# The first batch's opening: order of loads, who adds two half tiles, and block 0's scores in two groups

## The chip, the cores and the metric

The program runs on one core of one Trainium2 chip. The time is device microseconds (us) of the whole program, the median of three runs; a trace of one further execution is read beside it. On a core, TensorE (PE in the profile) multiplies matrices into PSUM, VectorE (DVE), ScalarE (ACT) and GpSimd (POOL) work elementwise, and SyncE (SP) issues the DMAs. Each engine works through its own instructions in order.

## What is computed

Four batches of attention over spatially reduced keys, followed by a small MLP on each batch's best 128 rows:

```
kv_pool = kv.reshape(B, H//4, 4, W//4, 4, C).mean(axis=(2, 4))    # 16 taps to one row
k = v = kv_pool.reshape(B, -1, C) @ w_sr                          # 768 keys a batch
s = (q @ k.T) / sqrt(C); a = exp(s - s.max(-1)); a /= a.sum(-1) + 1e-9
x = a @ v                                                         # 12288 rows a batch
out = x; out[top 128 rows by x @ w_gate] += sigmoid(x @ w_gate) * (relu(x @ w1) @ w2)
```

B is 4, C is 128; q has 12288 rows in each batch, kv has 384 x 32 positions.

## The kernel before

**Tiling.** The 768 keys of a batch are six tiles of 128. A tile's raw data (`kv_raw`, 128 channels x 2 halves x 64 keys x 16 taps, 1 MB) is added over the 16 taps into `pooled` (128 x 128). `project` (line 150) multiplies `pooled` by `w_k` (the keys, transposed) and by `w_sr` (the values) into one PSUM bank. ACT copies that to `kv_proj`, and each key tile is split for exactness into `kh` (a 32-bit matmul type), `kb` and `kl` (bf16: the value itself and what `kh` misses): `split_k` (line 154), two ACT casts and one POOL subtraction. Queries are split likewise by `split_q` (line 319) into `qh` (ACT) and `ql` (POOL), for two blocks at a time.

**Blocks.** The 192 blocks of 256 queries run in one loop. `S` (line 332) makes the scores of a block, 2 x 768 columns, as four parts of three matmuls each (`qh` x `kh`, `qb` x `kl`, `ql` x `kb`). `s_max` is one DVE reduction over all 1536 columns into `m`; ACT takes the exponential; the probabilities are cut into a high and a low half (`hl`, ACT and POOL), turned by DMA transposes and partly by PE (`turn_pe`, which is why `ident` in `cst` is needed), and `AV` multiplies them with the values four blocks later (`LAG` is 4). The values need scales from the whole batch first: `v_gate` (a product with the gate's weights, kept in `cst`), `v_max` and `v_peak` on DVE, then `v_split`, which writes `vx`.

**The opening, batch 0** (`first_keys`, line 214, called at line 604). Here DVE alone adds the tiles, half a tile (64 keys) an instruction. Batches 1 to 3 get theirs in the loop by `next_keys`, where POOL adds in seven instructions a tile. `first_values` (line 251) is a task whose steps the loop takes at named points: its first step at "g" of block 0, after `s_max(0)`, its second at "d" at the end of block 0, ahead of `s_max(1)`.

**What sets the order.** `InOrder` (line 37) ties every PE, DVE, ACT and POOL instruction to the one before it in the program's text, so that an engine never takes a later instruction ahead of an earlier one. The DMAs that SP issues stand in the text's order too. Buffers order the rest: `kv_raw` has three (`kvp`), so tiles 3, 4 and 5 are loaded into the buffers of tiles 0, 1 and 2 and the load waits until those have been read; `pooled` has two (`kvs`), so tile 4's sum is written where tile 2's was, and waits for tile 2's projection. Accesses to one PSUM bank of a tile are also put in order. `warm` (line 210) issues filler matmuls on PE, whose results nobody reads. In the page and the trace nearly every instruction has line 52, the helper's.

Of the kernel before, what the change touches and what calls it, by code (L numbers as in the profile page):

```python
# [6 lines left out]
F32 = mybir.dt.float32  # L7
# [6 lines left out]
AF = mybir.ActivationFunctionType  # L14
ALU = mybir.AluOpType
AX = mybir.AxisListType
# [3 lines left out]
P = 128  # L20
# [3 lines left out]
KT = M // P  # L24
TAPS = R * R
CHUNK = 2048
# [3 lines left out]
BLK = QT * P  # L30
# [36 lines left out]
def attention_topk_mlp(ctx, tc, a, outs, capacity):  # L67
    nc = tc.nc
    pe, dve, act, pool = (InOrder(tc, e) for e in (nc.tensor, nc.vector, nc.scalar, nc.gpsimd))
    SK = 1.0 / float(C) ** 0.5 / TAPS  # L70

    const = ctx.enter_context(tc.tile_pool(name="const", bufs=1))
    kvp = ctx.enter_context(tc.tile_pool(name="kvp", bufs=3))
    kvs = ctx.enter_context(tc.tile_pool(name="kvs", bufs=2))
# [10 lines left out]
    ps_o = ctx.enter_context(tc.tile_pool(name="ps_o", bufs=1, space=PSUM))  # L85

    w_sr = const.tile([P, C], F32, name="w_sr")
    nc.sync.dma_start(out=w_sr, in_=a["w_sr"])
    w_k = const.tile([P, C], F32, name="w_k")
    act.activation(w_k, w_sr, AF.Copy, scale=SK)  # L90
    cst = const.tile([P, 5 * P], F32, name="cst")
    ident, tri, jrow, wg = (cst[:, i * P:(i + 1) * P] for i in range(4))
    jcol, base = cst[:, 4 * P:4 * P + 1], cst[:, 4 * P + 1:4 * P + 3]
# [2 lines left out]
    tri16 = const.tile([P, P], BF16, name="tri16")  # L96
# [3 lines left out]
    s_flat = [x.rearrange("p k q -> p (k q)") for x in s_buf]  # L100
# [3 lines left out]
    banks = [o_two[:, j] for j in range(QT)]  # L104
# [14 lines left out]
    def load_kv(b, kc, parts=1, t=None):  # L119
        late = t is not None  # L120
        if not late:
            t = kvp.tile([P, 2, P // 2, TAPS], F32, name="kv_raw")
        n = 2 // abs(parts)
        for i in range(abs(parts)):
            if parts > 0 or late == (i > 0):
                nc.sync.dma_start(out=t[:, i * n:(i + 1) * n], in_=a["kv"][:, b, kc, i * n:(i + 1) * n])
        return t

    qraw = {}

    def load_q(b, ch, lo=0, hi=CHUNK):
        if (b, ch) not in qraw:
            qraw[b, ch] = qp.tile([P, CHUNK], F32, name="q_raw")
        nc.sync.dma_start(out=qraw[b, ch][:, lo:hi], in_=a["q"][:, b, ch, lo:hi])
# [3 lines left out]
    def new_keys(b):  # L138
        kvset[b] = {
            "kh": keys.tile([P, M], F32R, name="kh"),  # L140
            "kl": keys.tile([P, M], BF16, name="kl"),
            "kb": keys.tile([P, M], BF16, name="kb"),
            "raw": keys.tile([P, KT, 2, P], F32, name="kv_proj"),
            "vw": keys.tile([P, KT], F32, name="vw"),
            "mx": keys.tile([P, 4], F32, name="mx"),
            "vx": keys.tile([P, 2, KT, VC], F16, name="vx"),
            "sg": keys.tile([P, 4], F32, name="sg"),
        }

    def project(pooled, ps):  # L150
        pe.matmul(ps[:, 0], w_k, pooled, start=True, stop=True)
        pe.matmul(ps[:, 1], pooled, w_sr, start=True, stop=True)

    def split_k(b, lo, hi, part):
        kv = kvset[b]
        kh, kl, kb = (kv[k][:, lo * P:hi * P].rearrange("p (t k) -> p t k", k=P) for k in ("kh", "kl", "kb"))
        raw = kv["raw"][:, lo:hi, 0]
        if part == 0:
            act.copy(kh, raw)
            act.copy(kb, raw)  # L160
        else:
            kv["split"] = hi
            pool.tensor_tensor(out=kl, in0=raw, in1=kh.bitcast(F32), op=ALU.subtract)

    def v_gate(b, kc, v=None):
        u = kvs.tile([P, C], F32, name="vw_prod")
        dve.scalar_tensor_tensor(out=u, in0=kvset[b]["raw"][:, kc, 1] if v is None else v, scalar=1.0, in1=wg, op0=ALU.mult, op1=ALU.mult, accum_out=kvset[b]["vw"][:, kc:kc + 1])

    def v_max(b, pair):
        kv = kvset[b]  # L170
        dve.tensor_reduce(out=kv["mx"][:, pair:pair + 1], in_=kv["raw"][:, 2 * pair:2 * pair + 2, 1], axis=AX.XY, op=ALU.max, apply_absolute_value=True)

    def v_peak(b):
        mx, vw = kvset[b]["mx"], kvset[b]["vw"]
        dve.tensor_reduce(out=mx[:, 0:1], in_=mx[:, 0:3], axis=AX.X, op=ALU.max)
        dve.tensor_reduce(out=mx[:, 1:2], in_=vw, axis=AX.X, op=ALU.max, apply_absolute_value=True)
# [33 lines left out]
    def warm(n, ps):  # L210
        for _ in range(n):
            pe.matmul(ps, ones16, ones16, start=True, stop=True)

    def first_keys():
        new_keys(0)
        load_q(0, 0, 0, 2 * BLK)
        raws = [load_kv(0, kc) for kc in range(3)]
        nc.sync.dma_start(out=cst, in_=a["cst"])
        raws += [load_kv(0, kc, 2) for kc in range(3, KT)]
        load_q(0, 0, 2 * BLK, CHUNK)  # L220
        split_q(0, 0)
        kv = kvset[0]
        for kc in range(KT):
            pooled = kvs.tile([P, P], F32, name="pooled")
            for h in range(2):
                dve.tensor_reduce(out=pooled[:, h * P // 2:(h + 1) * P // 2], in_=raws[kc][:, h], axis=AX.X, op=ALU.add)
            if kc == 4:
                dve.tensor_copy(tri16, tri)
            if kc > 1:
                v_gate(0, kc - 2)  # L230
            if kc == 3:
                v_max(0, 0)
            ps = banks[kc % 2][:, 0:2 * P].rearrange("p (a b) -> p a b", a=2)
            if kc < KT - 1:
                project(pooled, ps)
                act.copy(kv["raw"][:, kc], ps)
                split_k(0, kc, kc + 1, 0)
                split_k(0, kc, kc + 1, 1)
            else:
                warm(4, banks[0][:, 0:P])  # L240
                project(pooled, ps)
                kh, kl, kb = (kv[k][:, kc * P:(kc + 1) * P] for k in ("kh", "kl", "kb"))
                dve.tensor_copy(kh, ps[:, 0])
                act.copy(kb, ps[:, 0])
                dve.tensor_tensor(out=kl, in0=ps[:, 0], in1=kh.bitcast(F32), op=ALU.subtract)
                act.copy(kv["raw"][:, kc, 1], ps[:, 1])
                warm(8, banks[1][:, 0:P])
        S(0)
        S(1)

    def first_values():
        yield "g"
        v_gate(0, KT - 2)
        v_max(0, 1)
        yield "d"
        v_gate(0, KT - 1)
        v_max(0, 2)
        v_peak(0)
        yield from v_split(0)

# [54 lines left out]
    qsplit = {}  # L315
# [3 lines left out]
    def split_q(b, blk):  # L319
        ch, h = divmod(blk, BPC)  # L320
        raw = qraw[b, ch][:, h * BLK:(h + 2) * BLK]
        qh = qs.tile([P, 2 * BLK], F32R, name="qh")
        ql = qs.tile([P, 2 * BLK], BF16, name="ql")
        act.copy(qh, raw)
        pool.tensor_tensor(out=ql, in0=raw, in1=qh.bitcast(F32), op=ALU.subtract)
        for i in range(2):
            h, l = (x[:, i * BLK:(i + 1) * BLK] for x in (qh, ql))
            qsplit[b, blk + i] = h, h.bitcast(BF16).rearrange("p (q s) -> p q s", s=2)[:, :, 1], l
# [3 lines left out]
    def S(n, parts=(0, 1, 2, 3), apart=()):  # L332
        b, blk = blocks[n]
        kh, kl, kb = (kvset[b][x] for x in ("kh", "kl", "kb"))
        qh, qb, ql = qsplit[b, blk]
        assert b == 0 or kvset[b].get("split") == KT
        for part in parts:
            lo, hi, j, k0 = ((0, 512, 0, 0), (512, 768, 0, 512), (768, 1024, 1, 0), (1024, 1536, 1, 256))[part]
            q = slice(j * P, (j + 1) * P)
            k = slice(k0, k0 + hi - lo)  # L340
            low, high = [(qb, kl), (ql, kb)], [(qh, kh)]
            for i, (w, x) in enumerate(high + low if part in (2, 0) else low + high):
                r = pe.matmul(s_flat[n % 2][:, lo:hi], w[:, q], x[:, k], start=(i == 0), stop=(i == 2))
                for y in apart:
                    tc.declare_no_dep(r.ins, y, reason="other banks")
# [256 lines left out]
    blocks = [(b, blk) for b in range(B) for blk in range(NBLK)]  # L602

    first_keys()
    nc.sync.dma_start(out=w1, in_=a["w1"])
    nc.sync.dma_start(out=w2, in_=a["w2"].rearrange("(t f) d -> f t d", f=P))
# [12 lines left out]
    def at_point(point):  # L619
        advance(vals, point)  # L620
        advance(prep, point)
        advance(select, point)

    start(vals, first_values())
    nb = len(blocks)
    LAG = 4
    for i in range(nb):
        old = i >= LAG
        b, blk = blocks[i]
# [56 lines left out]
    b = blocks[n][0]  # L686
# [168 lines left out]
    for m in range(n - 3, n + 1):  # L855
        out(m)
        norm(m)
        if m > n - 2:
            lo = blocks[m][1] * QT
# [99 lines left out]
```

## Time and profile before

| | |
|---|---|
| median of 3 runs | 961.53 us (959.38 to 965.91) |
| the profiled execution's own time | 964.65 us |
| its span | 962.7 us |
| mean granted TensorE clock | 0.991 |
| busy: PE, ACT, POOL, DVE | 93%, 78%, 78%, 71% |

A row of the timeline gives the start, the time (of all instructions merged into the row), the engine, the line, the operation and what it writes and reads with its shape; in brackets stands how long the engine was idle before it and what ended that. A merged row ("x2") begins with its first instruction. A granted clock of 1.00 is TensorE's full speed. The span begins at the first instruction, which is also where the stretches below are counted from.

### The profile page before, as it was taken

How to read it: one execution, taken by the hardware profiler on the slowest of the kernel's cores; microseconds unless marked ns; L12 is line 12 of the kernel's file. 1: busy time of each engine (PE TensorE's matmuls, PEld its weight loads, DVE VectorE, ACT ScalarE, POOL GpSimd, SP SyncE). 2: the span in 40 equal slices, each digit the busy share in tenths (PEclk: the TensorE clock that was granted, in tenths of full speed). 3: DMA queues.
4: the chain of work that ended last, by engine and by line, in shares of the span. 5: the costliest groups of instructions: out<-in, count | busy, mean ns of one | idle time of the engine just before them, and what ended most of it. 6: DMA issues, size and time to landing. Idle time of an engine off the chain costs nothing.

```text
span 962.7 us, 25910 instructions
## 1 busy us (share of the span) xinstructions
PE 894.8 (93%) x10093; PEld 730.6 (76%) x10093; DVE 686.0 (71%) x1575; ACT 754.1 (78%) x1181; POOL 753.7 (78%) x577
## 2 busy tenths in 40 slices
PE   3889999998999999999899999999999999899976
PEld 2668887787777777888687877888778877688765
DVE  6446666675777777787757877787777878688743
ACT  2568888786888777888788888888888988799941
POOL 1478898887798887899779989898878787588752
PEclk9999999999999999999999999999999999999999
DMA  9799999999989999999999999999999999999990
GB/s 361 211 206 207 240 240 221 230 233 236 218 178 217 236 211 236 238 217 236 240 193 205 215 238 236 225 206 205 197 206 205 238 239 232 223 252 224 231 179 27
DMA packets 600574, 211.47 MB, mean 220 GB/s; under 512 B 532320, under 2 KB 582624, under 8 KB 599680
## 3 DMA queue, kind: packets, MB, share of 16 engines
q1 hardware_dynamic: 600128, 209.12, 106.2%
q8 instruction: 80, 1.31, 0.6%
q0 software_dynamic: 320, 0.66, 0.2%
q14 instruction: 46, 0.38, 0.1%
HBM read 52.10 MB, written 25.49 MB: 81 GB/s over the span
## 4 chain that ended last, share of the span: by engine, by line
PE 56%; DMA 12%; ACT 9%; issue 6%; POOL 6%; DVE 5%; SPq 0%; POOLq 0%; DVEq 0%; another core or an unknown queue 0%; ACTq 0%
PE s L52 30%; PE o_two L52 26%; DMA at<-hl 12%; ACT am L52 4%; DVE m L52 2%; ACT hl L52 2%; POOL hl L52 2%; POOL ql L52 2%; POOL kv_sum L52 2%; DMA xe<-out,idx 1%; ACT qh L52 1%; DVE kv_raw L52 1%; ACT s L52 0%; POOL out L52 0%; ACT at L52 0%
## 5 line engine op out<-in xcount | busy, mean ns | idle before, releaser
L52 POOL TENSOR_TENSOR hl<-am,hl 128x1280 bf16<-128x1280 f32 x192 | 504.5, 2628 | 149.2 <-ACT hl L52 62.6
L52 PEld LDWEIGHTS <-at 128*128 128x128 f16 (+1 forms) x6912 | 417.2, 97 | 77.9 <-DMA at<-hl 28.0
L52 PE MATMUL o_two<-vx,at 128*128 128x130 f16 x6804 | 435.7, 220 | 24.1 <-DMA at<-hl 18.4
L52 ACT ACTIVATE am<-s,m 128x512 f32<-128x512 f32 (+1 forms) x528 | 358.5, 707 | 59.9 <-DVE m L52 34.4
L52 DVE TENSOR_REDUCE m<-s 128x2 f32<-128x1536 f32 x192 | 337.1, 1756 | 35.7 <-PE s L52 35.3
L52 PE MATMUL s<-kl,qh 128*128 128x512 bf16 (+1 forms) x768 | 253.4, 333 | 0.0
L52 PE MATMUL s<-kh,qh 128*128 128x512 f32 (+1 forms) x768 | 251.8, 409 | 1.5 <-DVE mg L52 1.5
L52 PE MATMUL s<-kb,ql 128*128 128x512 bf16 (+1 forms) x768 | 248.6, 327 | 2.3 <-POOL ql L52 1.8
L52 ACT CAST hl<-am 128x1280 f16<-128x1280 f32 x192 | 241.9, 1260 | 6.1
L52 PEld LDWEIGHTS s<-kh,qh 128*128 128x128 f32 x768 | 131.5, 191 | 31.6 <-DVE mg L52 1.9
L52 DVE TENSOR_TENSOR at<-s,at 128x256 bf16<-128x256 f32 x144 | 61.2, 425 | 103.1 <-ACT at L52 95.5
L52 POOL TENSOR_TENSOR ql<-q_raw,qh 128x512 bf16<-128x512 f32 x96 | 122.5, 1276 | 7.0 <-ACT qh L52 7.0
L52 PEld LDWEIGHTS <-qh 128*128 128x128 bf16 x768 | 75.3, 98 | 62.7 <-issue 61.8
L52 ACT CAST at<-s 128x256 f16<-128x256 f32 x144 | 53.6, 372 | 75.7 <-PE s L52 75.7
L52 DVE TENSOR_TENSOR x<-o_two,rz 128x260 f32<-128x260 f32 x189 | 81.0, 429 | 10.0
L52 PEld LDWEIGHTS <-ql 128*128 128x128 bf16 x768 | 76.2, 99 | 8.4 <-POOL ql L52 5.6
L52 DVE TENSOR_SCALAR rz<-o_two,sg 128x2 f32<-128x2 f32 x189 | 41.0, 217 | 39.6 <-PE o_two L52 39.2
L52 PE MATMUL s<-cst,am 128*128 128x128 f32 x288 | 56.4, 278 | 6.2 <-ACT am L52 5.8
L52 ACT CAST qh<-q_raw 128x512 fp32r<-128x512 f32 x96 | 59.0, 615 | 1.3 <-DMA q_raw<-in_q 1.3
L52 POOL TENSOR_TENSOR kv_sum<-kv_raw 128x256 f32<-128x256 f32 x72 | 52.3, 727 | 0.0
L52 PEld LDWEIGHTS s<-cst,am 128*128 128x128 f32 x288 | 34.5, 141 | 14.7 <-ACT am L52 13.2
L52 DVE RECIPROCAL rz<-rz 128x2 f32<-128x2 f32 x192 | 31.9, 166 | 6.6
(156 smaller groups left out, 502.7 us busy)
## 6 DMA issues: line engine op xcount, KB each, us to landing
out<-x SPq DMA_DIRECT2D x96, 256.0 KB, 2.9
q_raw<-in_q SPq DMA_DIRECT2D x93, 256.0 KB, 3.5
kv_raw<-in_kv SPq DMA_DIRECT2D x36, 512.0 KB, 6.4
kv_raw<-in_kv SPq DMA_DIRECT2D x6, 1024.0 KB
at<-hl SPq DMA_TRANSPOSE x384, 3.9
w<-in_w SPq DMA_DIRECT2D x2, 512.0 KB
q_raw<-in_q SPq DMA_DIRECT2D x1, 768.0 KB
cst<-in_cst SPq DMA_DIRECT2D x1, 320.0 KB
```

The costliest lines, as they stand in the source:

```text
L52: r = f(*args, **kwargs)
```

## The change

All of it lies in `first_keys` and `first_values`. Tile 0's first half is loaded ahead of all else, then `w_sr`, tile 0's second half, tiles 1 and 2, and only then the first 512 query columns. The later loads (more queries, `cst`, and behind them `w1`, `w2` and what the loop loads) stand behind a DVE memset into the query buffer that follows tile 4's addition. (The title of the change counts from one: its tile five is `kc` 4 here.) POOL adds the second half of tiles 2 and 3 in four instructions each. `split_q(0, 0)` moves behind tile 1's split. `v_gate`, `v_max` and `tri16` move out of the tile loop into `first_values`. Fillers, twelve a tile, follow the projections of tiles 1 to 4. Block 0's scores against tiles 0 to 3 (1024 of the 1536 columns) are issued after tile 4's projection, and the other 512 columns, against tiles 4 and 5, after tile 5's. Tile 5's key is projected twice, into two PSUM banks, and its value into a third, so that DVE and ACT read different banks.

```diff
@@ -85,9 +85,7 @@
     ps_o = ctx.enter_context(tc.tile_pool(name="ps_o", bufs=1, space=PSUM))
 
     w_sr = const.tile([P, C], F32, name="w_sr")
-    nc.sync.dma_start(out=w_sr, in_=a["w_sr"])
     w_k = const.tile([P, C], F32, name="w_k")
-    act.activation(w_k, w_sr, AF.Copy, scale=SK)
     cst = const.tile([P, 5 * P], F32, name="cst")
     ident, tri, jrow, wg = (cst[:, i * P:(i + 1) * P] for i in range(4))
     jcol, base = cst[:, 4 * P:4 * P + 1], cst[:, 4 * P + 1:4 * P + 3]
@@ -213,48 +211,94 @@
 
     def first_keys():
         new_keys(0)
+        raws = [kvp.tile([P, 2, P // 2, TAPS], F32, name="kv_raw") for _ in range(3)]
+        half = P // 4
+
+        def load(kc, h, lo=0, hi=P // 2):
+            nc.sync.dma_start(out=raws[kc][:, h, lo:hi], in_=a["kv"][:, 0, kc, h, lo:hi])
+
+        load(0, 0)
+        nc.sync.dma_start(out=w_sr, in_=a["w_sr"])
+        load(0, 1)
+        for kc in 1, 2:
+            nc.sync.dma_start(out=raws[kc], in_=a["kv"][:, 0, kc])
         load_q(0, 0, 0, 2 * BLK)
-        raws = [load_kv(0, kc) for kc in range(3)]
-        nc.sync.dma_start(out=cst, in_=a["cst"])
-        raws += [load_kv(0, kc, 2) for kc in range(3, KT)]
-        load_q(0, 0, 2 * BLK, CHUNK)
-        split_q(0, 0)
+        for kc in range(3, KT):
+            raws.append(kvp.tile([P, 2, P // 2, TAPS], F32, name="kv_raw"))
+            load(kc, 0)
+            if kc < KT - 1:
+                load(kc, 1)
+            else:
+                load(kc, 1, 0, half)
+                load(kc, 1, half, 2 * half)
+        act.activation(w_k, w_sr, AF.Copy, scale=SK)
         kv = kvset[0]
+        free = s_flat[1][:, 0:P]
+
+        def first(groups):
+            for lo, hi, j, k0, high_first in groups:
+                kh, kl, kb = (kv[x][:, k0:k0 + hi - lo] for x in ("kh", "kl", "kb"))
+                qh, qb, ql = (x[:, j * P:(j + 1) * P] for x in qsplit[0, 0])
+                low = [(ql, kb), (qb, kl)]
+                for i, (w, x) in enumerate([(qh, kh)] + low if high_first else low + [(qh, kh)]):
+                    pe.matmul(s_flat[0][:, lo:hi], w, x, start=(i == 0), stop=(i == 2))
+
         for kc in range(KT):
             pooled = kvs.tile([P, P], F32, name="pooled")
-            for h in range(2):
-                dve.tensor_reduce(out=pooled[:, h * P // 2:(h + 1) * P // 2], in_=raws[kc][:, h], axis=AX.X, op=ALU.add)
-            if kc == 4:
-                dve.tensor_copy(tri16, tri)
-            if kc > 1:
-                v_gate(0, kc - 2)
-            if kc == 3:
-                v_max(0, 0)
-            ps = banks[kc % 2][:, 0:2 * P].rearrange("p (a b) -> p a b", a=2)
+            pieces = [(h, 0, P // 2) for h in range(2)]
+            if kc == KT - 1:
+                pieces[1:] = [(1, 0, half), (1, half, 2 * half)]
+            if kc in (2, 3):
+                pieces.pop()
+                t, u = raws[kc][:, 1], kvs.tile([P, P // 2, TAPS // 2], F32, name="kv_sum")
+                for o, x, y in ((u, t[:, :, 0:8], t[:, :, 8:16]), (u[:, :, 0:4], u[:, :, 0:4], u[:, :, 4:8]),
+                                (u[:, :, 0:2], u[:, :, 0:2], u[:, :, 2:4]), (pooled[:, P // 2:], u[:, :, 0], u[:, :, 1])):
+                    pool.tensor_tensor(out=o, in0=x, in1=y, op=ALU.add)
+            for h, lo, hi in pieces:
+                dve.tensor_reduce(out=pooled[:, h * P // 2 + lo:h * P // 2 + hi], in_=raws[kc][:, h, lo:hi], axis=AX.X, op=ALU.add)
+            if kc == KT - 2:
+                dve.memset(qraw[0, 0][:, 2 * BLK:2 * BLK + 1], 0.0)
+                load_q(0, 0, 2 * BLK, 4 * BLK)
+                nc.sync.dma_start(out=cst, in_=a["cst"])
+                load_q(0, 0, 4 * BLK, CHUNK)
             if kc < KT - 1:
+                ps = banks[kc % 2][:, 0:2 * P].rearrange("p (a b) -> p a b", a=2)
                 project(pooled, ps)
+                if kc:
+                    warm(12, free)
                 act.copy(kv["raw"][:, kc], ps)
                 split_k(0, kc, kc + 1, 0)
                 split_k(0, kc, kc + 1, 1)
+                if kc == 1:
+                    split_q(0, 0)
+                if kc == KT - 2:
+                    first([(0, 512, 0, 0, True), (768, 1024, 1, 0, False), (1024, 1280, 1, 256, True)])
+                    warm(10, free)
             else:
-                warm(4, banks[0][:, 0:P])
-                project(pooled, ps)
+                kps, again, vps = banks[1][:, 0:P], banks[0][:, 0:P], s_flat[1][:, 512:512 + P]
+                pe.matmul(kps, w_k, pooled, start=True, stop=True)
+                pe.matmul(again, w_k, pooled, start=True, stop=True)
+                pe.matmul(vps, pooled, w_sr, start=True, stop=True)
+                warm(2, free)
                 kh, kl, kb = (kv[k][:, kc * P:(kc + 1) * P] for k in ("kh", "kl", "kb"))
-                dve.tensor_copy(kh, ps[:, 0])
-                act.copy(kb, ps[:, 0])
-                dve.tensor_tensor(out=kl, in0=ps[:, 0], in1=kh.bitcast(F32), op=ALU.subtract)
-                act.copy(kv["raw"][:, kc, 1], ps[:, 1])
-                warm(8, banks[1][:, 0:P])
-        S(0)
+                dve.tensor_copy(kh, kps)
+                act.copy(kb, again)
+                dve.tensor_tensor(out=kl, in0=kps, in1=kh.bitcast(F32), op=ALU.subtract)
+                act.copy(kv["raw"][:, kc, 1], vps)
+        first([(512, 768, 0, 512, True), (1280, 1536, 1, 512, True)])
         S(1)
 
     def first_values():
         yield "g"
-        v_gate(0, KT - 2)
+        for kc in range(3):
+            v_gate(0, kc)
+        v_max(0, 0)
+        yield "d"
+        for kc in range(3, KT):
+            v_gate(0, kc)
         v_max(0, 1)
-        yield "d"
-        v_gate(0, KT - 1)
         v_max(0, 2)
+        dve.tensor_copy(tri16, tri)
         v_peak(0)
         yield from v_split(0)
```

## Rows read from the trace of the kernel before

**Rows 1.** The page: busy time of PE with its share of the span, and the chain of work that ended last, by engine.

```profile
PE 894.8 (93%) x10093; PEld 730.6 (76%) x10093; DVE 686.0 (71%) x1575; ACT 754.1 (78%) x1181; POOL 753.7 (78%) x577
...
PE 56%; DMA 12%; ACT 9%; issue 6%; POOL 6%; DVE 5%; SPq 0%; POOLq 0%; DVEq 0%; another core or an unknown queue 0%; ACTq 0%
```

**Rows 2.** The chain of work that ended last, in order of time: start, us, what. The first is the earliest piece that it lists, the second its longest transpose.

```profile
55.22 3.08 PE o_two L52 x27
...
161.88 8.28 DMA at<-hl
```

**Rows 3.** Timeline of all engines, where block 0's probabilities meet the values for the first time: POOL's last piece of `vx`, and PE behind it.

```profile
54.52 0.65 POOL L52 TENSOR_TENSOR vx<-kv_proj,vx 128x256 f16<-128x256 f32 x1
...
55.22 3.08 PE L52 MATMUL o_two<-vx,at 128*128 128x130 f16 x27 [2.23 <-POOL vx L52]
```

**Rows 4.** Timeline of all engines from block 0's maximum to block 1's exponential.

```profile
30.20 1.76 DVE L52 TENSOR_REDUCE m<-s 128x2 f32<-128x1536 f32 x1 [5.40 <-PE s L52]
...
31.99 1.05 ACT L52 ACTIVATE am<-s,m 128x512 f32<-128x512 f32 x2 [6.38 <-DVE m L52]
...
32.58 1.18 PE L52 MATMUL o_two<-ones 128*128 128x128 bf16 x18
...
33.59 0.39 PE L52 MATMUL s<-cst,am 128*128 128x128 f32 x2
...
34.42 0.42 DVE L52 TENSOR_TENSOR at<-s,at 128x256 bf16<-128x256 f32 x1 [1.93 <-ACT at L52]
34.76 0.28 DVE L52 SCALAR_TENSOR_TENSOR vw_prod<-kv_proj,cst 128x128 f32<-128x128 f32 x1
...
34.97 0.41 DVE L52 TENSOR_REDUCE mx<-kv_proj 128x1 f32<-128x256 f32 x1
...
35.68 1.75 DVE L52 TENSOR_REDUCE m<-s 128x2 f32<-128x1536 f32 x1
...
37.47 1.05 ACT L52 ACTIVATE am<-s,m 128x512 f32<-128x512 f32 x2 [0.98 <-DVE m L52]
```

**Rows 5.** SP's queue: the loads of tiles 0 to 2 and of tiles 3 to 5, and the DMA view of the first 24 us, GB/s in 40 slices of 0.6 us.

```profile
1.67 1.37 SPq L126 DMA_DIRECT2D kv_raw<-in_kv  x3
...
9.48 5.90 SPq L126 DMA_DIRECT2D kv_raw<-in_kv  x6
...
GB/s 0 0 5 132 154 420 314 355 423 382 410 437 437 423 437 437 437 437 321 413 427 403 416 416 416 416 396 437 362 423 403 416 440 396 461 376 423 378 335 314
```

**Rows 6.** Timeline of DVE: its additions of tiles 0, 2 and 5, two instructions a tile.

```profile
7.11 2.34 DVE L52 TENSOR_REDUCE pooled<-kv_raw 128x64 f32<-128x1024 f32 x2 [7.11 <-DMA kv_raw<-in_kv]
...
12.20 2.35 DVE L52 TENSOR_REDUCE pooled<-kv_raw 128x64 f32<-128x1024 f32 x2 [0.23 <-DMA kv_raw<-in_kv]
...
20.16 2.33 DVE L52 TENSOR_REDUCE pooled<-kv_raw 128x64 f32<-128x1024 f32 x2
```

**Rows 7.** Timeline of all engines: the first query split, and what follows tile 0's addition (projection on PE, copy, the second cast of the key, and POOL's `kl`).

```profile
4.17 0.62 ACT L52 CAST qh<-q_raw 128x512 fp32r<-128x512 f32 x1 [1.27 <-DMA q_raw<-in_q]
4.87 1.26 POOL L52 TENSOR_TENSOR ql<-q_raw,qh 128x512 bf16<-128x512 f32 x1 [3.80 <-ACT qh L52]
...
9.60 0.77 PE L52 MATMUL o_two<-pooled,w_k 128*128 128x128 f32 x2 [9.60 <-DVE pooled L52]
...
10.83 0.37 ACT L52 COPY kv_proj<-o_two 128x256 f32<-128x256 f32 x1 [6.04 <-PE o_two L52]
...
11.44 0.29 ACT L52 CAST kb<-kv_proj 128x128 bf16<-128x128 f32 x1
11.61 0.46 POOL L52 TENSOR_TENSOR kl<-kv_proj,kh 128x128 bf16<-128x128 f32 x1 [5.48 <-ACT kh L52]
```

**Rows 8.** Groups of POOL instructions by shape: busy us, mean ns of one, idle before.

```profile
L52 POOL TENSOR_TENSOR kv_sum<-kv_raw 128x256 f32<-128x256 f32 x72 | 52.3, 727 | 0.0
L52 POOL TENSOR_TENSOR kv_sum<-kv_sum 128x512 f32<-128x512 f32 x18 | 23.0, 1278 | 0.0
...
L52 POOL TENSOR_TENSOR kv_sum<-kv_sum 128x256 f32<-128x256 f32 x18 | 11.1, 618 | 0.0
...
L52 POOL TENSOR_TENSOR pooled<-kv_sum 128x128 f32<-128x128 f32 x18 | 7.6, 425 | 0.0
...
L52 POOL TENSOR_TENSOR vx<-vw,vx 128x6 f16<-128x6 f32 x4 | 1.0, 256 | 0.0
```

**Rows 9.** PE around block 0's scores, in order of time (eight fillers, three matmuls of block 0, three of block 1), and, last, one stretch of the view of stretches: start and end, us, busy us and instructions of PE, PEld, DVE, ACT and POOL, granted clock, DMA share, GB/s.

```profile
25.15 1.01 PE L52 MATMUL o_two<-ones 128*128 128x128 bf16 x8 [1.37 <-ACT kv_proj L52]
...
25.92 0.78 PE L52 MATMUL s<-kh,qh 128*128 128x512 f32 x1
...
26.50 0.65 PE L52 MATMUL s<-kl,qh 128*128 128x512 bf16 x1
...
26.94 0.63 PE L52 MATMUL s<-kb,ql 128*128 128x512 bf16 x1
...
30.83 0.54 PE L52 MATMUL s<-kb,ql 128*128 128x512 bf16 x1
...
31.91 0.38 PE L52 MATMUL s<-kl,qh 128*128 128x512 bf16 x1
...
32.12 0.38 PE L52 MATMUL s<-kb,ql 128*128 128x512 bf16 x1
...
25.00:30.00 5.00, 4.85 (x21) 3.22 (x20) 0.00 (x0) 0.61 (x2) 1.27 (x1) 1.00 1.03 418
```

## The prediction

> **What bounds the kernel now.** I read the page first, then the chain of waits, then the timeline of the first 60 us. PE is busy for 93% of the span, and 56% of the chain is PE with 12% in the DMA transposes [rows 1]. But the listed chain begins only at 55.22, where PE takes up block 0's values [rows 2]. From there on PE sets the time, and nothing in the change touches that part. So the change is worth what it moves 55.22 by.
>
> What releases PE there is POOL's last `vx`, at 54.52 [rows 3]; that follows the chain of blocks 1 to 3 on ACT and POOL, which starts with block 1's exponential at 37.47. ACT had waited 0.98 us for that, for DVE's maximum of block 1 at 35.68 [rows 4]. I take the 19.5 us from 35.68 to 55.22 as unchanged: **the time moves with the start of block 1's maximum.** That one waits for DVE's order: block 0's maximum (30.20), the cut of block 0's probabilities (34.42), a few small value instructions [rows 4]. And block 0's maximum waited for the scores, which waited for tile 5.
>
> **The change part by part.** "Tile n" is `kc` n.
>
> *Loads.* A full stream ran from 3.0, some 1.3 us after the first large load was issued at 1.67, and brought about 0.40 MB/us at first; tile 0's reduction began at 7.11, 0.95 after the 1.38 MB up to tile 0 had moved at about 6.15 [rows 5, 6]. With a large load issued first, at about 0.73, I start the stream at 2.05: tile 1 (2.16 MB in) lands at 2.05 + 5.45 + 0.95 = 8.5. If the slow start is bound to time, not to the size of the first load, it is 9.0. By the same sum tile 2 lands at about 11 and the 512 queries 0.6 later. DVE has tile 1 added at 8.5 + 2.35 = 10.85 [rows 6].
>
> *The half tiles on POOL.* This decides. POOL's order in the text is `kl` of tile 0, `kl` of tile 1, `ql`, additions of tile 2, `kl` of tile 2, additions of tile 3, `kl` of tile 3. Nothing may pass. From a tile added to its `kl` ended took 9.45 to 12.07, 2.62 us, and to its `kb` ended 2.28 [rows 7]. So `kl` of tile 1 ends at 13.5, `qh` runs on ACT from 13.15, and `ql`, which before came 0.70 after `qh`'s start and took 1.26 [rows 7], ends at 15.1. Tile 2 has then been in memory for 4 us.
>
> Price of one half tile, 64 x 8, 64 x 4, 64 x 2 and 64 x 1 elements: 512 from `kv_raw` lies between 1.278 (512 from `kv_sum`) and 1.454 (twice 727 ns); I take 1.39, the 727 ns plus the step from 256 to 512 in the other shape. Then 0.62, 0.425, and 0.34 between 0.256 and 0.425 [rows 8]. Sum 2.8. Ends: 2.6 if all shapes go at the cheaper row, 3.3 with the dearer ones and a short wait between dependent instructions, which no row shows. What DVE did in 1.17 [rows 6] takes POOL 2.8. The Trainium skill, GPSIMD Engine Reference, section 3.1 (Elementwise), gives about 2.6 cycles an element at 1.2 GHz for a two-input operation, an estimate of 2.1 us for these 960 elements without dispatch; by it the sum below would be 1.4 us less.
>
> So tile 2 is added at 15.1 + 2.8 = 17.9, its `kl` ends at 20.5, tile 3 is added at 23.3, its projection (1.35 from addition to copy [rows 7]) ends at 24.65. Tile 4 has been added meanwhile (DVE writes it into tile 2's `pooled`, free at 19.25, ready by 21.6). Tile 5's buffer comes free after POOL's first addition of tile 2, at 16.5; its loads land by about 21, and its sum needs tile 3's `pooled`, free at 24.65, so it is ready at 27.1, against 22.5 before [rows 6]. The early load is given back here.
>
> *PE.* After tile 3's projection stand, in order: 12 fillers, tile 4's projection, 12 fillers, block 0's first 1024 columns, 10 fillers, three 32-bit products of tile 5, 2 fillers, 512 columns. At the speed of the opening: a filler 0.126 (1.01 for 8), a projection 1.23 (so 1.85 for three), all 1536 columns 25.92 to 30.20, or 4.28 [rows 4, 7, 9]. That is 1.51 + 1.23 + 1.51 + 2.85 + 1.26 + 1.85 + 0.25 + 1.43 = 11.9 us. Tile 5's sum at 27.1 and its casts lie beneath this: PE gets to them later. What speeds it is the clock. The granted clock reads 1.00 in that stretch, yet 512-column matmuls came 0.44 apart (26.50, 26.94), and 0.21 apart at 31.91: the lower of the two levels, 1.2 GHz, then 2.4. The change lies just after 30.83, 5.7 us after PE's unbroken work began at 25.15 [rows 9]. Here unbroken work begins with tile 3's projection at 23.45, so I put the rise at 29.15: 4.5 us of the 11.9 done, the other 7.4 in 3.7. Block 0's maximum starts at 24.65 + 4.5 + 3.7 = 32.85. Ends: all at 2.4 GHz, 30.6; none, 36.55.
>
> *To block 1's maximum.* Before, 5.48 us after block 0's. There PE's transposes (33.59) came after block 1's scores and 18 fillers [rows 4]; at 2.4 GHz those are done earlier and the transposes wait for the exponential (0.45 gained). `first_values` adds to DVE, ahead of block 1's maximum, two `v_gate` (0.21 to 0.37, say 0.29), one `v_max` (0.44) and `tri16` (0.15): 1.17. Three `v_gate` and a `v_max` more lie in DVE's pause before 34.42 and cost nothing while that pause (1.93 us) holds. So 6.2, and block 1's maximum starts at 39.05 against 35.68.
>
> *At nothing:* the memset (one column); the held loads, which move about 4 us later but have until block 0's transposes; `w_k`, since `w_sr` lands just after the first half; and the second key product, counted in PE's three.
>
> **Sum:** +3.4 us. The profiled execution's own 964.65 would become 968.0; it lies 3.1 above the median, so on the median 961.53 + 3.4 = 964.9, rounded to **965**.
>
> **Rivals.** *A, faster: loads and additions overlap as drawn.* Should POOL add tile 2 as it lands (11), everything is paced by the loads: the last lands at about 19.2, tile 5 is added at 19.8, tile 4 at 16.9. PE then has 1.35 + 1.51 + 2.85 + 1.26 to do behind tile 4 and 3.5 behind tile 5: block 0's maximum at 25 to 27.4, block 1's at 31.2 to 33.6, 2 to 4.5 us earlier: about 958. Against it: `ql` and `kl` stand ahead of the additions in the text, and the helper keeps that order. For it: DVE, which had no pause between tiles 2 and 5 [rows 6], is relieved of all its small work.
>
> *B, slower: PE stays at 1.2 GHz through the opening.* All 11.9 us count, block 0's maximum is at 36.55 and block 1's 6.65 later: 7.5 us over, 969. It decides if PE's work between 23.45 and the late scores has pauses, as the opening's work had before. The Trainium skill, TensorE: Matmul & The Clock Gate, part 1, has the clock rise only after sustained activity; the trace agrees, since the short projections before left PE at 0.44 apart [rows 9].
>
> *C, slower by over 1%: a new phase of the transposes.* A shift of the start moves loads against DMA transposes; pieces of up to 8.28 us hang on these in the chain [rows 2]. Two more such pieces would give 10 us or more, 972 and up. Nothing in the stretch around the change speaks for it.
>
> **How the numbers follow.** The forecast 0.65 (with PE at 2.4 GHz throughout: +1.1; POOL at 3.3: +1 on top of +3.4); A 0.15; B 0.14; C 0.04; 0.02 left for a shift that gains as much as C loses. What can't be told from no change is 1%, 9.6 us: 951.9 to 971.1. The forecast, A and B all lie in that: same 0.93, faster 0.02, slower 0.05. The range takes in A's middle and B, 958 to 970; the forecast's own is 962 to 967.
>
> **What the changed profile would show.** DVE's first reduction near 4.5; POOL starting on tile 2 only after `ql`, near 15, with PE idle until about 18; tile 3's projection after 23; fillers 0.126 apart before some point and 0.06 after; block 0's maximum near 33, 6.2 before block 1's; the first `vx` piece on PE near 58.6. I am wrong if POOL starts tile 2 by 12, if the four additions take under 2 us, or if PE has its scores before 28.

## The result and the profile after

The changed kernel took 969.71 us (median of 11 runs, 963.1 to 973.82) against 963.78 us for the kernel before in its 11 runs. The ratio over all runs is 1.0059, 95% interval 1.0032 to 1.0087, so **5.7 us slower (3.1 to 8.4)**. Ratios here and below leave out slow executions: one of e1's 12 (1987 us), one of e2's 12 (1511 us) and one of the kernel before (969.65 us). The time lies in the range of the prediction (958 to 970), near its upper end; the forecast was +3.4. That range was reckoned from 961.53, the median of three runs. From 963.78 the forecast gives 967.2 and rival B, +7.5, gives 971.3: the measured time lies between them, so only the trace can tell which of the two happened.

The page of the changed kernel, the same lines as [rows 1]: less of the chain is PE, more is DVE, ACT and issue.

```profile
PE 889.4 (92%) x9965; PEld 734.5 (76%) x10146; DVE 684.3 (71%) x1575; ACT 753.8 (78%) x1181; POOL 758.7 (79%) x585
...
PE 50%; DMA 12%; ACT 11%; issue 8%; DVE 7%; POOL 6%; SPq 0%; POOLq 0%; DVEq 0%; another core or an unknown queue 0%; ACTq 0%
```

The chain of waits of the changed kernel again begins where PE takes up block 0's values, now at 60.08 instead of 55.22 [rows 2]. (That is PE's start on the rest of these products, behind the last piece of `vx`. It had begun on the first pieces at 50.22, now 55.09, which is the same shift.) **The opening is 4.86 us longer**, which lies within the interval of the measured difference.

```profile
60.08 3.08 PE o_two L52 x27
```

The timeline of the changed kernel's opening, all engines, the instructions that carried the prediction:

```profile
9.37 2.34 DVE L52 TENSOR_REDUCE pooled<-kv_raw 128x64 f32<-128x1024 f32 x2 [1.48 <-DMA kv_raw<-in_kv]
...
13.87 0.46 POOL L52 TENSOR_TENSOR kl<-kv_proj,kh 128x128 bf16<-128x128 f32 x1 [3.36 <-ACT kh L52]
...
14.59 1.26 POOL L52 TENSOR_TENSOR ql<-q_raw,qh 128x512 bf16<-128x512 f32 x1 [0.26 <-ACT qh L52]
15.81 1.25 POOL L52 TENSOR_TENSOR kv_sum<-kv_raw 128x512 f32<-128x512 f32 x1
17.14 1.20 POOL L52 TENSOR_TENSOR kv_sum<-kv_sum 128x256 f32<-128x256 f32 x2
18.42 0.30 POOL L52 TENSOR_TENSOR pooled<-kv_sum 128x64 f32<-128x64 f32 x1
18.77 0.50 PEld L52 LDWEIGHTS o_two<-pooled,w_k 128*128 128x128 f32 x2 [4.71 <-POOL pooled L52]
...
20.09 2.34 DVE L52 TENSOR_REDUCE pooled<-kv_raw 128x64 f32<-128x1024 f32 x2 [5.05 <-PE o_two L52]
...
20.81 0.46 POOL L52 TENSOR_TENSOR kl<-kv_proj,kh 128x128 bf16<-128x128 f32 x1 [2.09 <-ACT kh L52]
21.22 1.25 POOL L52 TENSOR_TENSOR kv_sum<-kv_raw 128x512 f32<-128x512 f32 x1
...
24.19 0.79 PE L52 MATMUL o_two<-pooled,w_k 128*128 128x128 f32 x2 [2.92 <-POOL pooled L52]
...
25.50 2.40 DVE L52 TENSOR_REDUCE pooled<-kv_raw 128x64 f32<-128x1024 f32 x3 [3.06 <-issue]
```

Tile 1 is added by 11.7, and tile 2's data are there (DVE takes the first half at 11.93). POOL takes the second half at 15.81, behind `kl` and `ql`; PE's weight load (PEld) waits 4.7 us for it, and DVE 5.1 us for the projection behind it. DVE adds tile 5 at 25.5 to 27.9, where the kernel before was done at 22.5 [rows 6].

From block 0's maximum on, the same lines as [rows 4]:

```profile
33.22 1.76 DVE L52 TENSOR_REDUCE m<-s 128x2 f32<-128x1536 f32 x1 [0.73 <-PE s L52]
...
36.91 0.43 DVE L52 TENSOR_TENSOR at<-s,at 128x256 bf16<-128x256 f32 x1 [0.96 <-ACT at L52]
37.25 0.28 DVE L52 SCALAR_TENSOR_TENSOR vw_prod<-kv_proj,cst 128x128 f32<-128x128 f32 x1
...
38.93 1.75 DVE L52 TENSOR_REDUCE m<-s 128x2 f32<-128x1536 f32 x1
...
38.96 0.53 PE L52 MATMUL s<-cst,mx 128*128 128x128 f32 x2 [2.50 <-ACT hl L52]
...
39.29 3.74 PE L52 MATMUL o_two<-ones 128*128 128x128 bf16 x36
...
40.71 1.05 ACT L52 ACTIVATE am<-s,m 128x512 f32<-128x512 f32 x2 [1.74 <-DVE m L52]
...
44.30 0.37 ACT L52 CAST at<-s 128x256 f16<-128x256 f32 x1 [2.54 <-PE s L52]
```

PE pauses for 2.50 us before 38.96. Then block 1's 36 fillers take 3.74 us. In the kernel before, the pause was 1.74 us and the same fillers took 2.17:

```profile
35.72 0.42 PE L52 MATMUL s<-cst,mx 128*128 128x128 f32 x2 [1.74 <-DVE mx L52]
35.98 2.17 PE L52 MATMUL o_two<-ones 128*128 128x128 bf16 x36
```

The pause grew by 0.76 us, as much as DVE's value work between the cut of block 0's probabilities and block 1's maximum (0.92 us from 34.76 to 35.68 [rows 4], now 1.68 from 37.25 to 38.93). The view of stretches says why the fillers were slow: the granted clock falls to 0.57, so most of that stretch ran at the lower of the two levels, 1.2 GHz.

```profile
39.00:43.00 4.00, 4.00 (x38) 3.91 (x40) 2.00 (x3) 1.05 (x2) 3.36 (x4) 0.57 0.39 88
```

### The profile page after: what moved, and what is told of

The parts are those of the page before. It is cut to its first block, busy times and chain, and to the rows that moved or that the text cites. A ratio compares the mean times of both kernels' runs of the same rounds, so it can differ in the third digit from the quotient of the medians.

```text
span 963.9 us, 25850 instructions
## 1 busy us (share of the span) xinstructions
PE 889.4 (92%) x9965; PEld 734.5 (76%) x10146; DVE 684.3 (71%) x1575; ACT 753.8 (78%) x1181; POOL 758.7 (79%) x585
## 4 chain that ended last, share of the span: by engine, by line
PE 50%; DMA 12%; ACT 11%; issue 8%; DVE 7%; POOL 6%; SPq 0%; POOLq 0%; DVEq 0%; another core or an unknown queue 0%; ACTq 0%
PE s L52 27%; PE o_two L52 23%; DMA at<-hl 11%; ACT am L52 5%; DVE m L52 4%; ACT hl L52 3%; POOL ql L52 2%; POOL hl L52 2%; POOL kv_sum L52 2%; ACT s L52 1%; ACT qh L52 1%; DMA q_raw<-in_q 1%; DVE kv_raw L52 1%; DVE hl L52 0%; DVE idx L52 0%
## 5 line engine op out<-in xcount | busy, mean ns | idle before, releaser
L52 PE MATMUL s<-kb,ql 128*128 128x256 bf16 (+1 forms) x698 | 221.0, 320 | 7.6 <-POOL ql L52 1.6
L52 PE MATMUL s<-kl,qh 128*128 128x256 bf16 (+1 forms) x659 | 210.5, 323 | 0.1
L52 POOL TENSOR_TENSOR kv_sum<-kv_raw 128x256 f32<-128x256 f32 (+1 forms) x74 | 54.9, 742 | 0.0
L52 POOL TENSOR_TENSOR kv_sum<-kv_sum 128x256 f32<-128x256 f32 (+2 forms) x40 | 36.3, 907 | 0.3
```

What stands on the lines that cost most here:

```text
L52: r = f(*args, **kwargs)
```

## The experiments

The opening is read from one profiled execution of each kernel: the start of block 0's, block 1's and block 5's maximum (block 5's is the first one behind the meeting with the values) against the profiled execution of the kernel before, which had them at 30.20, 35.68 and 60.73. Ratios are to the kernel before in the same sessions, from 7 to 12 runs of each kernel and 30 to 35 of the kernel before (11 and 11 for the changed kernel).

| kernel | block 0's, us | block 1's | block 5's | ratio (95%) |
|---|---|---|---|---|
| as changed | +3.0 | +3.3 | +4.7 | 1.0059 (1.0032 to 1.0087) |
| e1 DVE adds all | -4.9 | -4.7 | -2.0 | 0.9975 (0.9951 to 0.9999) |
| e2 POOL early | -3.5 | -3.3 | -0.6 | 1.0033 (1.0009 to 1.0056) |
| e2 again | -2.2 | -2.0 | -0.4 | 1.0010 (0.9984 to 1.0036) |
| e3 fillers in block 0 | +3.0 | +3.2 | +4.0 | 1.0039 (1.0010 to 1.0067) |
| e4 no fillers | +2.6 | +2.8 | +4.3 | 1.0086 (1.0055 to 1.0116) |
| e5 best so far | -5.3 | -5.5 | -5.5 | 0.9973 (0.9952 to 0.9994) |
| e6 old loads | -5.1 | -4.9 | -5.1 | 0.9994 (0.9969 to 1.0020) |
| e7 whole scores | -4.9 | -4.7 | -3.3 | 0.9982 (0.9958 to 1.0006) |
| e8 DVE, no fillers | -3.9 | -3.6 | -3.5 | 1.0003 (0.9971 to 1.0035) |
| e9 before + fillers | -1.2 | -1.7 | -0.6 | 1.0040 (1.0010 to 1.0071) |
| e10 before again | -0.4 | -0.9 | +0.1 | 1.0013 (0.9989 to 1.0037) |
| e11 best, clock kept | -5.3 | -5.5 | -7.1 | 0.9957 (0.9930 to 0.9983) |

### POOL's order or POOL's work (e1, e2)

DVE adds everything:

```diff
-            if kc in (2, 3):
-                pieces.pop()
...
-                    pool.tensor_tensor(out=o, in0=x, in1=y, op=ALU.add)
```

> The changed kernel with DVE adding all of every tile, POOL nothing (the rest as changed). Theory (POOL's order: its additions stand behind kl and ql, and kl behind its additions): the chain is gone. DVE adds a tile in 2.35, tile 2 by 14.3; tile 5's last piece is added near 21, when its load has landed, against 27.9. PE's work is then unbroken from tile 1's projection (11.9) on, so its clock rises near 17.6; block 0's maximum starts near 24 instead of 33.2, block 1's near 30 instead of 38.9, PE meets the values near 51 instead of 60.1. Against the kernel before (55.2) some 4 to 5 us faster, ratio 0.995. Rival (the loss lies in PE's own new work and in DVE's value work, not in POOL): block 0's maximum moves by 2 us at most, and the time stays 4 to 6 us over the kernel before, ratio 1.005.

POOL keeps its halves, but they come ahead of what it would have to wait for (`half_on_pool` holds the four additions):

```diff
                 split_k(0, kc, kc + 1, 0)
+                if kc in (1, 2):
+                    half_on_pool(kc + 1)
                 split_k(0, kc, kc + 1, 1)
-                if kc == 1:
+                if kc == 2:
                     split_q(0, 0)
```

> The changed kernel with POOL's additions kept but put ahead of the waiting instructions: tile 2's before kl of tile 1, tile 3's before kl of tile 2, and the query split behind tile 2's. Theory (it is POOL's order, not POOL's work as such): tile 2 is added from its landing, 11.9 to 14.7, tile 3's half from 15.1 to 17.9, tile 5 near 21.5; block 0's maximum near 24 to 25, PE meets the values near 51 to 52, ratio 0.995, as with DVE adding all. Rival (POOL's 2.75 us for a half tile is the loss wherever it stands): block 0's maximum not before 29, ratio 1.0 or more.

e1, DVE's timeline: tiles 2 and 3 in one go from 11.89, tile 5 done at 22.1 and not at 27.9, block 0's maximum at 25.28 instead of 33.22.

```profile
11.89 4.60 DVE L52 TENSOR_REDUCE pooled<-kv_raw 128x64 f32<-128x1024 f32 x4 [0.25 <-DMA kv_raw<-in_kv]
17.19 2.35 DVE L52 TENSOR_REDUCE pooled<-kv_raw 128x64 f32<-128x1024 f32 x2 [0.69 <-DMA kv_raw<-in_kv]
...
19.70 2.41 DVE L52 TENSOR_REDUCE pooled<-kv_raw 128x64 f32<-128x1024 f32 x3 [0.15 <-DMA kv_raw<-in_kv]
...
25.28 1.76 DVE L52 TENSOR_REDUCE m<-s 128x2 f32<-128x1536 f32 x1 [0.73 <-PE s L52]
```

In e2 PE waits 0.51 and 0.79 us for POOL's sums instead of 4.4 and 2.9, tile 5 is added at 22.0, and block 0's maximum starts at 26.70; in the second execution (e2 again) at 27.97.

```profile
15.02 0.79 PE L52 MATMUL o_two<-pooled,w_k 128*128 128x128 f32 x2 [0.51 <-POOL pooled L52]
...
18.31 0.79 PE L52 MATMUL o_two<-pooled,w_k 128*128 128x128 f32 x2 [0.79 <-POOL pooled L52]
```

So the theory holds: the halves on POOL cost 7.9 us to block 0's maximum, and moving the same four instructions ahead of `kl` and `ql` gives 5.3 to 6.5 of these back. The rest, 1.4 to 2.7, is POOL's longer time for a half tile (PE takes up tile 3 at 18.31, in e1 at 16.65) and a later rise of PE's clock. In time, the changed kernel and e1 lie apart beyond their intervals, by about 8 us, where block 5's maximum lies 6.7 apart; e2's gain over the changed kernel is within the scatter.

The expected ratio of e1, 0.995, was too good: values met at 51.90 instead of 51, and a ratio of 0.9975, whose interval just misses 1 (its median, 963.81, is not below the 963.45 of the kernel before). e2's time did not follow its opening at all, so it was measured once more.

> The kernel with POOL's additions put early, a second time. Its opening was 1.9 us shorter than that of the kernel before (values met at 53.3), its time 0.1 to 0.6% longer. If that difference belongs to the session, the ratio now comes out near 0.998; if to the kernel (a part behind the opening that lasts longer), near 1.003 again.

It came out between the two: 1.0010. Its interval holds 1.003 and just misses 0.998, so e2's time probably does not gain what its opening does.

### The lost clock in block 1 (e3)

```diff
             turn_pe(i)
+        if i == 0:
+            warm(36, banks[0][:, 0:P])
```

> The changed kernel with 36 more fillers on PE behind block 0's two transposes, in PE's pause from 36.5 to 39.0. Theory (PE's clock was granted at about half in 39 to 43 because PE paused for 2.5 us before it, and the 36 fillers of block 1 at 0.104 made block 2's scores and block 1's transposes late): the maxima of block 0 and 1 stay at 33.2 and 38.9, block 1's fillers take 2.2 us instead of 3.7, block 1's turned probabilities are copied near 42.7 instead of 44.3, and PE meets the values near 58.5 instead of 60.1; time 1.5 us less than the changed kernel, ratio to the kernel before 1.004. Rival (POOL's own order sets the meeting with the values, whatever the clock): copied earlier, but the values still met near 60.

The maxima of blocks 0 and 1 stayed (33.20, 38.91), the same stretch kept its clock, the values were met at 58.44:

```profile
39.00:43.00 4.00, 4.00 (x50) 3.52 (x50) 1.99 (x2) 1.39 (x4) 3.37 (x4) 1.00 0.41 92
...
58.44 3.08 PE L52 MATMUL o_two<-vx,at 128*128 128x130 f16 x27 [2.23 <-POOL vx L52]
...
61.81 1.20 PE L52 MATMUL s<-kh,qh 128*128 128x512 f32 x2
```

1.64 us of the 4.86 are this clock. Not all of it stays: at block 5's maximum 0.7 is left (64.73 against 65.46). Behind the meeting the scores in e3 still ran at the lower level (the last line; the changed kernel has 0.70 there), so part was lost again. In time e3 (1.0039) can't be told from the changed kernel (1.0059). The fall is not certain: of the eight profiled executions with that pause of 2.50 (the changed kernel, e1, e2 twice, e4, e6, e7, e8) six lost the clock, and e6 and e8 kept it. In the six block 2's maximum came 6.8 to 7.1 us after block 1's, in those two and in all other kernels 5.4.

### Fillers (e4, e8, e9)

e4: the changed kernel without them.

```diff
-                if kc:
-                    warm(12, free)
...
-                    warm(10, free)
...
-                warm(2, free)
```

> The changed kernel without the fillers of the opening (12 behind each of tiles 1 to 4, 10 behind the early scores, 2 behind tile 5's products). The late tiles come as before (tile 3's projection at 24.2). If the fillers only bring the clock up: PE stays at 1.2 GHz, from 25.4: 1.23 + 2.85 + 1.85 + 1.43 plus the waits for the casts, so block 0's maximum is near 33, no change, and block 1's scores take 0.44 a 512-column matmul; block 1's maximum near 39.5, ratio 1.006. Rival (the fillers stand in the way): block 0's maximum is 2 us or more earlier, 31 or less, and the ratio falls below 1.004.

Block 0's maximum at 32.79, 0.4 earlier, as expected: there the fillers cost about what their clock gives. The ratio, 1.0086 from 7 runs, lies above the opening's shift by 4 us, which the trace of the opening does not explain.

e8: the same edit on e1.

> DVE adding all tiles, without any of the opening's fillers. Theory (the fillers raise PE's clock in the opening and that is the gain): tile 5 is added at 22 as with them, but PE stays at 1.2 GHz: early scores until 23.7, three products 1.85, late scores 1.43 and the casts, so block 0's maximum is near 27.3 instead of 25.3. Rival (the clock hardly counts, as with POOL's chain, where leaving the fillers out cost nothing): block 0's maximum stays near 25.3.

26.33, 1.05 us later than with fillers, half of what was expected: without fillers too the clock had risen before the last group. Matmuls of 256 columns stand 0.21 apart in the early scores (22.21, 22.42) and 0.12 in the last group (25.90, 26.02). Behind it there was no lost clock in block 1 either, so that its values were met at 51.58, 0.3 earlier than e1's.

e9: fillers alone, in the kernel before.

```diff
                 project(pooled, ps)
+                if kc:
+                    warm(12, s_flat[1][:, 0:P])
```

> The kernel before with one part of the change alone: 12 fillers behind the projections of tiles 1 to 4. Theory (the fillers' clock is what the change brings): PE at full clock from about 18; tile 5 is added at 22.5 as before, its projection takes 0.7 instead of 1.2, block 0's scores 2.15 instead of 4.3; block 0's maximum near 27.2 instead of 30.2, block 1's 5.0 later, near 32.2, and everything behind it 3.5 us earlier; ratio 0.9965. Rival (fillers delay the projections as much as they gain): block 0's maximum at 29.5 or later, ratio 1.0.

Block 0's maximum at 29.05: a gain of 1.15, not 3. PE did reach the higher level (tile 4's key projection took 0.46 instead of 0.76), but it then stood still for 1.37 us while tile 5 was cast, and the view of stretches has the clock down again just where block 0's scores run:

```profile
22.00:24.70 2.70, 0.72 (x5) 0.55 (x6) 1.34 (x5) 0.59 (x3) 0.00 (x0) 1.00 1.07 358
24.70:29.00 4.30, 4.30 (x21) 2.67 (x20) 0.00 (x0) 0.46 (x1) 1.26 (x1) 0.60 1.04 414
```

PE was busy for 0.72 us of the 2.70 before. A clock raised and not kept is worth little.

### What the other parts are worth (e6, e7)

e6: e1 with the loads of the kernel before; the memset and the later loads behind it go as well.

```diff
-        load(0, 0)
         nc.sync.dma_start(out=w_sr, in_=a["w_sr"])
-        load(0, 1)
-        for kc in 1, 2:
+        load_q(0, 0, 0, 2 * BLK)
+        for kc in range(3):
             nc.sync.dma_start(out=raws[kc], in_=a["kv"][:, 0, kc])
-        load_q(0, 0, 0, 2 * BLK)
+        nc.sync.dma_start(out=cst, in_=a["cst"])
...
+        load_q(0, 0, 2 * BLK, CHUNK)
```

> DVE adding all tiles, with the loads in the order of the kernel before (w_sr and queries first, tile 0 whole, cst behind tile 2, nothing held). Theory (the early loads are given back, because tiles 3 to 5 go into the buffers of tiles 0 to 2 and DVE adds at the loads' own pace): tile 0 is added 2.5 us later, but tile 2 lands near 12.2 instead of 11.9, and tile 5 is added near 22.5 instead of 22.1; block 0's maximum 0.4 later, near 25.7. Rival (the order of the loads is worth what tile 0 gains): tile 5 near 24, block 0's maximum near 27.

DVE's timeline: tile 0 at 6.97, where e1 began on its first half at 4.51; tile 2 at 12.08 instead of 11.89, tile 5 added at 22.5 instead of 22.1, as expected. Even that 0.4 is lost: block 0's maximum is 0.2 *earlier*. In e1 DVE waited 0.69 us for tile 4's load (its line at 17.19), here it did not. So PE took up tile 4 at 19.27 instead of 19.69, and the early scores, the 10 fillers and behind them tile 5's products (22.63 instead of 22.86) came earlier. The early loads are worth 0.4 us at most: tiles 3 to 5 land in buffers that come free only as DVE adds. (The values are met at 50.30, 1.6 before e1's: 0.2 of it is the earlier maximum, 1.4 the clock in block 1, kept here.)

```profile
6.97 2.34 DVE L52 TENSOR_REDUCE pooled<-kv_raw 128x64 f32<-128x1024 f32 x2 [6.97 <-DMA kv_raw<-in_kv]
...
12.08 7.04 DVE L52 TENSOR_REDUCE pooled<-kv_raw 128x64 f32<-128x1024 f32 x6 [0.26 <-DMA kv_raw<-in_kv]
...
25.07 1.76 DVE L52 TENSOR_REDUCE m<-s 128x2 f32<-128x1536 f32 x1 [0.73 <-PE s L52]
```

e7: e1 with all scores of block 0 behind tile 5's products.

```diff
-                    first([(0, 512, 0, 0, True), (768, 1024, 1, 0, False), (1024, 1280, 1, 256, True)])
...
-        first([(512, 768, 0, 512, True), (1280, 1536, 1, 512, True)])
+        first([(0, 512, 0, 0, True), (768, 1024, 1, 0, False), (1024, 1280, 1, 256, True), (512, 768, 0, 512, True), (1280, 1536, 1, 512, True)])
```

> DVE adding all tiles, with all of block 0's scores behind tile 5's products instead of two groups (fillers kept). PE is at full clock by then, so the 1024 columns cost 1.45 us and not 2.85, and 10 fillers no longer stand behind them, so tile 5's products start 0.7 earlier: block 0's maximum 0.7 later than with two groups, near 26.0. So of the 4.9 us between the kernel before (30.2) and DVE adding alone (25.3) the clock would bring most, the two groups 0.7. Rival (the two groups bring it): block 0's maximum at 28 or later.

25.30 against 25.28, where 0.7 was expected: with fillers, the two groups are worth nothing either. The 1024 columns fill PE's wait for tile 5's casts instead.

### The control and a version that beats both (e5, e10, e11)

e5 is e1 with e3's fillers, without the 10 fillers that held tile 5's products back, and with value work in DVE's pause:

```diff
-                    warm(10, free)
...
-        for kc in range(3):
+        for kc in range(5):
             v_gate(0, kc)
         v_max(0, 0)
+        dve.tensor_copy(tri16, tri)
         yield "d"
-        for kc in range(3, KT):
-            v_gate(0, kc)
+        v_gate(0, 5)
...
-        dve.tensor_copy(tri16, tri)
```

> The changed kernel with DVE adding all tiles, and three small edits: 36 fillers behind block 0's transposes, no 10 fillers behind the early scores, and the gate products of tiles 3 and 4 with the triangle's cast in DVE's pause before the cut of block 0's probabilities. If the costs found so far add up: block 0's maximum 0.55 earlier than with DVE adding alone (25.3), near 24.7; block 1's another 0.57 earlier, near 29.9 (31.0); block 1's fillers at full clock, 1.4 less; PE meets the values near 49.4 (51.9, and 55.2 in the kernel before): 5.8 us faster than the kernel before, ratio 0.994. Rival (what the opening gains is lost behind it): met near 49.4, but a ratio of 0.998 or more.

Values met at 49.73, near the expected 49.4, and the ratio 0.9973, between the expected 0.994 and the rival's 0.998: half of the opening's gain shows.

> The kernel before itself, as a control: ratio 1.000 within its interval. The experiments so far lie on average 2 us above what the shift of their openings gives; if that comes from how the runs are compared, the control comes out at 1.002.

The control: 1.0013, its interval holds both 1.000 and 1.002. Its own opening was 0.9 shorter at block 1 and 0.1 longer at block 5.

e11 is e5 with fillers inside block 0's first product with the values:

```diff
         for i, (w, h, kt) in enumerate(mm):
+            if n == 0 and j == 0:
+                warm({5: 6, 8: 16, 9: 30}.get(i, 0), banks[1][:, 0:P])
             pe.matmul(o, w[:, kt], vx[:, h, kt], start=(i == 0), stop=(i == len(mm) - 1))
```

> The best version so far (DVE adding, small edits) with 6, 16 and 30 fillers put into PE's three pauses inside block 0's first product with the values. There the clock fell to 0.5 in every kernel (27 matmuls in 3.08 us, 0.11 each). If the fillers keep it up: the 27 take about 1.6, the maximum of block 5, 5.5 us behind their start so far, comes 1.7 to 2 us earlier, near 53.4 (55.25 without, 60.7 in the kernel before): 7.3 us before the kernel before, ratio 0.995 by the shares seen so far. Rival (POOL's next probabilities bind there): block 5's maximum unchanged.

The 27 matmuls took 1.71 instead of 3.08, and block 5's maximum came at 53.67, 1.6 before e5's. **Ratio 0.9957, interval 0.9930 to 0.9983**: faster than the kernel before by about 4 us, and than the changed kernel by about 10. In time it can't be told from e5 (0.9973).

```profile
49.68 1.71 PE L52 MATMUL o_two<-vx,at 128*128 128x130 f16 x27 [0.57 <-POOL vx L52]
...
53.67 1.76 DVE L52 TENSOR_REDUCE m<-s 128x2 f32<-128x1536 f32 x1 [0.18 <-PE s L52]
```

## Why the prediction came out as it did

**Right: where the time is set.** The chain of waits begins at the meeting with the values in both kernels, and the shift of that point, 4.86, agrees with what the runs show, 5.7 (3.1 to 8.4). In the traces the shift against the kernel before stays within 0.2 us from block 5 to block 20, in all but one of the 13.

**Right: the step that decided, POOL's order.** `kl` of tile 1 ended at 14.33 (13.5 forecast), `ql` at 15.85 (15.1), tile 2 was added at 18.72 (17.9) and tile 3 at 24.14 (23.3), tile 5 at 27.9 (27.1). The constant 0.8 is the first term: tile 1 landed at 9.37, and I had taken 8.5, with 9.0 as the other end. The half tile took 2.91 from 15.81 to 18.72, against 2.8: the first addition was cheaper (1.25, not 1.39), and between dependent instructions POOL stood about 0.1, the wait that no row showed. The Trainium skill, GPSIMD Engine Reference, section 3.1 (Elementwise), had given an estimate of 2.1 us without dispatch; the trace decides for 2.9. e1 and e2 show the cause as such.

**Right: PE's clock before block 0's maximum,** forecast at 33, found at 33.22. The rise came at about 28.7 (the fillers up to there took 1.49 for 12, the early scores from 29.11 on are 0.23 apart), 4.5 us after PE's work began at 24.19 and not 5.7; that makes up for half of the 0.8. Rival B is out, since the late scores ran at the higher level. The Trainium skill, TensorE: Matmul & The Clock Gate, part 1, has the clock rise only after sustained activity; the trace agrees, with fillers and projections one behind the other from 24.19 to 28.7.

```profile
27.44 1.49 PE L52 MATMUL s<-ones 128*128 128x128 bf16 x12
...
29.11 0.39 PE L52 MATMUL s<-kb,ql 128*128 128x512 bf16 x1
29.34 0.38 PE L52 MATMUL s<-kl,qh 128*128 128x512 bf16 x1
```

**Too high by 0.5: block 0's to block 1's maximum,** 5.71 against 6.2. The value work ahead of block 1's maximum took 1.68 us (37.25 to 38.93); I had 0.92 plus 1.17. The products stand 0.21 apart, not 0.29, and the two `v_max` took 0.66 together, not 0.88. This miss and the 0.4 by which block 0's maximum came late (33.22 against 32.85) cancel: that block 1's maximum moved by 3.25, against 3.4 forecast, is partly luck.

**Wrong: "I take the 19.5 us from 35.68 to 55.22 as unchanged".** They became 21.15 (38.93 to 60.08). This is the step that failed, a term left out of the sum: PE's pause ahead of block 1 grew by the 0.76 us of added value work, its clock fell, most of block 1's fillers ran at 1.2 GHz, and block 2's scores stood behind them. Block 2's maximum came 7.06 us after block 1's; in the kernel before and in e3 it was 5.44. e3 prices the step at 1.64. I had asked about the clock in the opening alone (rival B) and not looked at what the longer order on DVE does to PE's next pause. With it the sum is 3.25 + 1.6, the 4.86 found.

**Rival A** as drawn: e2 has its order. Its maximum of block 0 came at 26.70 and 27.97 (25 to 27.4 forecast); the gain in time of some 3.5 us that the rival forecast did not come (ratios 1.0033 and 1.0010). That POOL is not needed at all was not among my cases: e1 gains more.

**Nothing, and said to be nothing:** the held loads and the memset. The early loads I had called "given back" by POOL; e6 shows that they bring nothing even without POOL. It takes out the held loads, the memset and the early loads together, so it does not price them one by one.

**A part that I had counted only as cost:** the second key product in another bank was to let DVE and ACT cast at the same time. It did not; `kb` began when `kh` was done and `kl` when `kb` was done, 0.32 and 0.30 us apart, as in the kernel before (23.88, 24.20, 24.50):

```profile
31.58 0.29 DVE L52 CAST kh<-o_two 128x128 fp32r<-128x128 f32 x1 [3.67 <-PE o_two L52]
31.90 0.27 ACT L52 CAST kb<-o_two 128x128 bf16<-128x128 f32 x1 [3.31 <-DVE kh L52]
...
32.20 0.29 DVE L52 TENSOR_TENSOR kl<-o_two,kh 128x128 bf16<-128x128 f32 x1 [0.33 <-ACT kb L52]
```

Both banks belong to one tile, `o_two`. That this is why they are put in order was not tried. For the scores the kernel lifts such an order by hand (`declare_no_dep`, "other banks"), which the change does not do here.

**Open:** the times lie above what the openings give. Over the 13 comparisons a fit of the time's difference on block 5's shift has a slope of 0.85, which its scatter does not tell from 1, and lies 2.2 us above zero at no shift (correlation 0.89); e2, e4, e6, e8 and e9 stand about 4 us above their openings. The control's 1.3 us, with an interval from -1.1 to 3.6, takes in the 2.2 but doesn't settle it. In the traces the shift against the kernel before wanders by 5 to 10 us behind block 24, and by 5.6 in the control, where pieces of DMA transposes stand in the chain [rows 2]. What causes it was not tried.

## What to carry to other kernels

Before handing an idle engine work, write down what already stands in its queue: here two half tiles of 2.9 us each cost 8, because their additions stood behind a `kl` that waited for a chain and in front of one that the chain waited for, and in another place they cost 1.4 to 2.7. A step that lengthens one engine's order also lengthens the pauses of the others, so look at what PE's clock does behind each pause, and put fillers where heavy matmuls follow one. Judge a change of an opening by the moment at which the steady part begins; block 5's maximum agreed within 0.2 us between the two executions of e2 and of the kernel before, while the whole time of one kernel scatters by 10 us, more than the change.

## What was not expected of the hardware

After the same pause of 2.50 us PE's clock fell in six executions and stayed in two; it fell in e9 behind a stretch with PE busy for 0.72 of 2.70 us, and stayed after the pause of 1.74 in the kernel before, e9 and e10. The same kernel's opening differed by 1.3 us between two executions (e2: block 0's maximum at 26.70 and 27.97): tile 1 landed 0.5 us later in the second (10.05 against 9.54), and the rest is that PE's clock rose later. And a load order that let DVE begin on tile 0's first half 2.5 us earlier brought tiles 1 and 2 in 0.2 earlier: between 5 and 8 us the loads moved 0.32 to 0.35 MB/us in e1 and 0.39 to 0.41 in e6. Why was not looked into.
